# A recurrent attention kernel with a feed-forward part: k and q projected chunk by chunk on one weight load, scores and attends regrouped

## The chip, the cores and the metric

The kernel runs on one core of one Trainium2 chip. The metric is the device time of one execution in microseconds (us).

## The reference

Two parts read the same input `x` (2048 tokens of 1024) and a sigmoid gate mixes them. Part A is recurrent: 64 segments of 32 tokens, each preceded by 8 memory rows that are the first 8 output rows of the segment before.

```python
for s in range(n_seg):                       # 64 segments, one after the other
    h = concat([mem, x[:, 32*s:32*s+32]])    # 8 + 32 rows of 1024
    q, k, v = h @ Wq, h @ Wk, h @ Wv         # 32 heads of 128
    scores = where(mask, q @ k.T * scale, -1e9)
    o = softmax(scores) @ v
    o = o @ Wo
    mem = o[:8]; outs.append(o[8:])
a = concat(outs)
b = (gelu(x @ w_gate) * (x @ w_up)) @ w_down # 1024 -> 3584 -> 1024
out = g * a + (1 - g) * b                    # g = sigmoid(x . gate_w)
```

The comparison with the reference says little about part A. With these inputs `g * a` has a standard deviation of 1.0e-5, the output one of 4.8e-3 (both computed from the reference with and without `Wo`).

## The kernel before

TensorE walks 64 weight chunks of 512 KB in each segment: for each half of the heads eight chunks of k, q, v and o. Most chunks stay in SBUF; twelve places are shared by the two halves ("paired"), so twelve chunks, 6.3 MB, are fetched again in each segment, each as soon as its place has been used. Gaps are filled with projections for later rows ("fills", f1 and f2), which do not hang on the recurrence.

```python
ORDER = (("k", 0), ("q", 0), ("v", 0), ("k", 1), ("q", 1), ("o", 0), ("v", 1), ("o", 1))
walk = [(m, r, i) for m, r in ORDER for i in seq(m, r)]
...
# sharing of bytes that matters below
a_bf = al("a_bf", [128, 256], at=pA.off)      # output rows of a segment; softmax result pA
vA = al("vA", [128, 4, 128], at=oT.off)
tA = al("tA", [128, 8, 32], at=qT.off)        # transposed probabilities
...
def scores(r):                                # TensorE, then the softmax on VectorE
    e.matmul(PB[SS][:, 0:320], lhsT=ident[:, :], rhs=mS..., start=True, stop=False)   # mask
    for lo, hi, c in ((0, 32, 0), (32, 40, 40)):          # 16 main, 16 tail products
        for j in range(4):
            for g in range(4):
                e.matmul(PB[SS][32*g : 32*g+hi-lo, ...], lhsT=qT[:, j, g, :] or qkr[...8 columns],
                         rhs=kT[:, j, g, :], start=False, stop=True)
    ... max, exp, sum, pA = E * 1/sum, tA = transpose(pA), pB, tB = transpose(pB)
...
# projection of a chunk: four 32-column tiles, 512 columns each, a weight load for each
for g in range(4):
    e.matmul(PB[bk][32*g:32*g+32, :], lhsT=h[:, i, :], rhs=w[:, g*512:(g+1)*512], ...)
...
# the second half's place in the segment
on("k", 1, 0, lambda: scores(0))
on("q", 1, 5, lambda: trans(kT))              # after five q chunks
on("o", 0, 0, lambda: evac(bank_of["q", 1], tok))
on("o", 0, 0, some(f1, 2)); on("o", 0, 0, lambda: attend(ua))
on("o", 0, 0, some(f1, 2)); on("o", 0, 0, lambda: attend_tail(ua))
on("o", 0, 0, some(f1, 1)); on("o", 0, 0, lambda: trans(qT))
...
on("o", 1, 3, lambda: fill_store(*k2, G, stage[1]))       # four v_scr stores, if k2 is a v fill
pend.append(store)                            # a_scr <- a_bf, issued early in the next segment
```

Of the kernel before, what the change touches and what calls it, by code (L numbers as in the profile page):

```python
# [195 lines left out]
def bass_gated_mix__memory_aug_recurrent_mem_tr__geglu_ffn__prompt_kernel(  # L196
# [30 lines left out]
    LQ = 40  # L227
    of = out.flatten_outer_dims()
    mem0 = A_mem0.flatten_outer_dims()

    with ExitStack() as es:
# [60 lines left out]
        oT = al("oT", [128, 4, 4, LQ])  # L292
        tok = al("tok", [128, 512])
        stage = [al(f"stg{n}", [128, 512]) for n in range(2)]
# [3 lines left out]
        vA = al("vA", [128, 4, 128], at=oT.off)  # L298
        tA = al("tA", [128, 8, 32], at=qT.off)
# [10 lines left out]
        part = al("part", [128, 256], FP32, at=odd0 + 1024)  # L310
        oR2 = al("oR2", [128, RB, 16], at=odd0 + 1024)
# [5 lines left out]
        def seq(m, r):  # L317
            p = [i for i in range(8) if i in PAIRS[m]]
            f = sorted((i for i in range(8) if i not in p), key=lambda i: (m == "k" and i % 2, i))
            return p + f if r == 0 else f + p  # L320
        ORDER = (("k", 0), ("q", 0), ("v", 0), ("k", 1), ("q", 1), ("o", 0), ("v", 1), ("o", 1))
        walk = [(m, r, i) for m, r in ORDER for i in seq(m, r)]

# [67 lines left out]
        for g in range(4):  # L391
            q = slice(32 * g, 32 * g + 32)


            pw(mS, lambda e, q=q: sel(e, mS[q, 0:NR], ALU.is_ge, NEG, 0, [[-1, NR]], 1))
            pw(mS, lambda e, q=q: sel(e, mS[q, 32:40], ALU.is_ge, NEG, -NR, [[0, NB]], 1))

            pw(mS, lambda e, q=q: sel(e, mS[q, 72:80], ALU.is_ge, NEG, 0, [[-1, NB]], 1))
# [26 lines left out]
        st0 = stage + [al(f"st0{i}", [128, 512], at=odd0 + 1024 * i) for i in range(2)]  # L425
        dl = al("dl", [128, NT], FP32, at=stage[1].off + stage[1].nb - 64)
# [24 lines left out]
        def pre_j(fb, j):  # L451
# [5 lines left out]
            if j == NJP - 1:  # L457
                slow.append(lambda: op("sp", lambda e: e.dma_start(g_scr[fb], g[:, :, :].rearrange("p j c -> p (j c)")), rd=[g.r()],
                                       wr=[("D", "g", fb)], lane=f"gw{fb % 2}"))
# [12 lines left out]
        def load_x(T):  # L472
            if T < NT:
                op("sp", lambda e: e.dma_start(px[T % NPX][:, :], xf[T * 128:(T + 1) * 128, :]), wr=[px[T % NPX].r()], lane=f"px{T % NPX}")
# [52 lines left out]
        load_x(0)  # L527
        op("act", lambda e: e.dma_start(gwb[:, :], gate_w.rearrange("(o d) -> o d", o=1).to_broadcast([128, D])),
           wr=[gwb.r()], lane="gw")
        for T in range(1, NPX):  # L530
            load_x(T)
# [34 lines left out]
        for fb in range(NFB):  # L566
            for j in range(NJP):
                T = TB * (fb + 1) + j
                now, puts[:], slow[:] = list(puts), slow, []
                if T < NT:  # L570
                    do_x(T)
                    load_x(T + NPX)
# [95 lines left out]
        def trans4(e, t=tok):  # L668
            for j in range(4):
                ins = e.transpose(PBV[TT][:, j * 128:(j + 1) * 128], t[:, j * 128:(j + 1) * 128], ident[:, :])  # L670
            return ins

        def trans(to):
            op("pe", trans4, rd=[tok.r(), ident.r()], wr=[BK(TT)])
# [7 lines left out]
        def scores(r, mid=None):  # L682

            def f(e):
                e.matmul(PB[SS][:, 0:320].rearrange("p (a c) -> p a c", a=4), lhsT=ident[:, :],  # L685
                         rhs=mS[:, :].unsqueeze(1).to_broadcast([128, 4, 80]), start=True, stop=False, skip_group_check=True)
                for lo, hi, c in ((0, 32, 0), (32, 40, 40)):
                    for j in range(4):
                        for g in range(4):
                            x = 8 * (4 * j + g)  # L690
                            ins = e.matmul(PB[SS][32 * g:32 * g + hi - lo, j * 80 + c:j * 80 + c + LQ],  # L691
                                           lhsT=qT[:, j, g, :] if lo == 0 else qkr[:, r, 0, x:x + 8], rhs=kT[:, j, g, :], start=False, stop=True, skip_group_check=True)
                return ins
# [24 lines left out]
        def attend(u):  # L718

            def f(e):  # L720
                for j in range(4):
                    for g in range(4):
                        r = slice(32 * g, 32 * g + 32)
                        ins = e.matmul(PB[bo[g]][:, j * LQ:(j + 1) * LQ], lhsT=vA[r, j, :],  # L724
                                       rhs=tA[r, 2 * j:2 * j + 2, :].rearrange("p a c -> p (a c)")[:, 0:LQ],
# [4 lines left out]
        def attend_tail(u):  # L730
            def f(e):
                for g in range(4):
                    r = slice(32 * g, 32 * g + 32)
                    ins = e.matmul(PB[bo[g]][:, 0:4 * LQ].rearrange("p (j c) -> p j c", j=4)[:, :, 24:40], lhsT=vB[r, u, :],  # L734
                                   rhs=tB[r, :, :].rearrange("p (j a) c -> p j (a c)", a=2)[:, :, 24:40],
# [3 lines left out]
            n = 4 * LQ  # L739
            for g in range(4):  # L740
                cp[("act", "dve")[g % 2]](oT[:, g, :, :].rearrange("p j c -> p (j c)"), PB[bo[g]][:, 0:n], [BK(bo[g])],
                                          [oT.r(g * n, (g + 1) * n)])
            op("pool", lambda e: e.tensor_copy(oRc[:, u, :, :].rearrange("p c x -> p x c"),  # L743
                                               oT[:, :, :, 32:40].rearrange("p g j c -> p (g j) c")),
               rd=[oT.r()], wr=[oRc.r(128 * u, 128 * u + 128)])

        bank_of = {("k", 0): B0, ("q", 0): B1, ("v", 0): B2, ("k", 1): B0, ("q", 1): F2, ("v", 1): B0}

        def proj(p, s):
            k = at_step(p, s)  # L750
            w = slots[home[k]]
            i = k[2]
            if k[0] != "o":
                h, bk = hTs[s % 2], bank_of[walk[p][:2]]

                def f(e):
                    for g in range(4):
                        ins = e.matmul(PB[bk][32 * g:32 * g + 32, :], lhsT=h[:, i, :], rhs=w[:, g * 512:(g + 1) * 512],  # L758
                                       start=(p % 8 == 0), stop=(p % 8 == 7))
                    return ins  # L760
                op("pe", f, rd=[h.r(32 * i, 32 * i + 32), w.r()], wr=[BK(bk)])
            else:
# [3 lines left out]
                def f(e):  # L766
                    for hh in range(2):
                        for g in range(4):
                            c = hh * 1024 + g * 256
                            ins = e.matmul(PB[XO][32 * g:32 * g + 32, 0:256], lhsT=oT[:, gp_, 2 * jj + hh, 0:32],  # L770
                                           rhs=w[:, c:c + 256], start=(r == 0 and p % 8 == 0 and hh == 0), stop=(r == 1 and p % 8 == 7 and hh == 1))
                    return ins
                n = 4 * LQ
# [42 lines left out]
        def fill_trans():  # L816
            op("pe", trans4, rd=[tok.r(), ident.r()], wr=[BK(TT)])
# [23 lines left out]
        def tr0(m, u, t, n, G=0):  # L841
            op("pe", lambda e: trans4(e, t), rd=[t.r(), ident.r()], wr=[BK(TT)])
            fill_put(st0[n], "dve")
            if G == 0:
                x = 256 * u + 128 * (m == "k")
                op("pool", lambda e: e.tensor_copy(qkr[:, u, 0 if m == "q" else 1, :], st0[n][:, 0:128]), rd=[st0[n].r(0, 128)],
                   wr=[qkr.r(x, x + 128)])
            fill_store(m, u, G, st0[n])
# [6 lines left out]
        base_of = {mr: 8 * n_ for n_, mr in enumerate(ORDER)}  # L855
# [3 lines left out]
        for s in range(NSEG):  # L859
# [12 lines left out]
            def on(m, r, n, *fs):  # L872
                at.setdefault(base_of[m, r] + n, []).extend(fs)
# [10 lines left out]
            if s == 0:  # L884
                on("k", 0, 0, lambda: mm0("v", 0, F1, st0[3]))
                on("k", 0, 0, lambda: mm0("k", 0, F2, tokB))
                if NG > 1:
                    on("k", 0, 0, lambda: mm0("k", 0, F1, tok, 1, hR1))
                    on("k", 0, 4, lambda: tr0("k", 0, tok, 1, 1))
                on("k", 0, 0, lambda: tr0("k", 0, tokB, 0))  # L890
                on("q", 0, 0, lambda: mm0("q", 0, F1, tokB))
                if NG > 1:
                    def q_next():
                        for f in fill("q", 0, F2, hR1):
                            f()
                        tr0("q", 0, tokB, 2)
                        act_copy(tokB[:, :], PB[F2][:, :], [BK(F2)], [tokB.r()])
                    on("q", 0, 0, q_next)
                    on("q", 0, 3, lambda: tr0("q", 0, tokB, 3, 1))
                else:  # L900
                    on("q", 0, 3, lambda: tr0("q", 0, tokB, 2))
                on("v", 0, 4, lambda: (rest_k(0), load_v(0, slice(0, 1))))

                def fills_1():
# [3 lines left out]
                    tr0("k", 1, tok, 1)  # L908
                    act_copy(tok[:, :], PB[F2][:, :], [BK(F2)], [tok.r()])
                    mm0("v", 1, F1, st0[2])  # L910
                    tr0("q", 1, tok, 3)
# [7 lines left out]
            on("q", 0, 0, lambda: evac(bank_of["k", 0], tok))  # L919
            on("q", 0, 5, lambda: trans(kT))  # L920
            on("v", 0, 0, lambda: evac(bank_of["q", 0], tok))
            on("v", 0, 5, lambda: trans(qT))
            on("k", 1, 0, lambda: evac(bank_of["v", 0], vA))
            on("k", 1, 0, lambda: scores(0))
            on("k", 1, 3, lambda: rest_k(1))
            on("q", 1, 0, lambda: evac(bank_of["k", 1], tok))
            on("q", 1, 5, lambda: trans(kT))

            def add_part():
                op("dve", lambda e: e.tensor_tensor(out=stage[0][:, 0:256], in0=PB[F1][:, 0:256], in1=part[:, :], op=ALU.add),  # L930
                   rd=[BK(F1), part.r()], wr=[stage[0].r(0, 256)])

            on("o", 0, 0, lambda: evac(bank_of["q", 1], tok))
            on("o", 0, 0, some(f1, 2))
            on("o", 0, 0, lambda: attend(ua))
            on("o", 0, 0, some(f1, 2))
            on("o", 0, 0, lambda: attend_tail(ua))
            on("o", 0, 0, some(f1, 1))
            on("o", 0, 0, lambda: trans(qT))
            on("o", 0, 0, some(f1))  # L940
            if k1:
                on("o", 0, 1, lambda: fill_evac(*k1, F1, stage[0]))
# [3 lines left out]
            if k1:  # L946
                on("o", 0, 6, fill_trans)
                on("o", 0, 6, lambda: fill_put(stage[0], "act"))
                on("o", 0, 6, lambda: fill_store(*k1, G, stage[0]))
            if uw == 0:  # L950
                on("o", 0, 6, lambda: store_tail(Q, stage[0]))
            on("o", 1, 0, lambda: evac(bank_of["v", 1], vA))
            on("o", 1, 0, some(f2, 4))
# [190 lines left out]
```

## Time and profile before

| | before |
|---|---|
| median of the first three runs (lowest, highest) | 2238.44 us (2237.15, 2244.4) |
| run with the profile | 2225.83 us, span 2224.0 |
| TensorE busy | 93% of the span |
| first segment ends / recurrence of 62 more / last segment and feed-forward part | 149.8 / 1511.6 / 562.6 us |
| TensorE's waits for instructions ("issue") | 60.0 us |

The recurrence is counted from the closing transposes of the first segment to those of the last; most of the argument is about it. The run with the profile was one of the faster ones, 12 us below the median. Waits: columns are the total in us, the number of waits and the longest.

```profile
DVE pA L704 <- DMA a_scr<-a_bf: 14.4, 16, 1.5
```

The softmax may write `pA` only when the store of `a_bf`, which shares its bytes, has landed. In 16 segments it came too late, and hardly a wait of TensorE follows from it: its waits for kT were 4.5 us in the whole recurrence.

### The profile page before, as it was taken

The numbers are of one execution on the slowest core, as the hardware profiler recorded it, in microseconds if no ns is written. First come the engines' busy times: TensorE is split into PE (matmuls) and PEld (weight loads), VectorE is DVE, ScalarE is ACT, GpSimd is POOL, SyncE is SP. The second block draws the span as 40 slices with busy tenths as digits, with TensorE's granted clock in tenths as the row PEclk, the third lists the DMA queues.
The fourth block names the chain that finished last, engine by engine and source line by source line (L and its number), as shares of the span: only waits on it lengthen the run. The fifth ranks groups of instructions, "written<-read, shape, count | busy, mean of one in ns | idle before, by whom it ended". The sixth has DMA issues, their size and how long they took to land.

```text
span 2224.0 us, 80042 instructions
## 1 busy us (share of the span) xinstructions
PE 2074.7 (93%) x36623; PEld 1096.6 (49%) x36642; DVE 905.1 (41%) x2152; ACT 610.6 (27%) x1296; POOL 617.9 (28%) x1139
## 2 busy tenths in 40 slices
PE   7879999999899999999999999999888999999999
PEld 3334555455555555555555555555444444444444
DVE  5433344334334343443344344334434516354362
ACT  4322322223232232323233232223222303122130
POOL 5123333432333334233333423333321000000000
PEclk9989999999999999999999999999999999999999
DMA  9977888788778888887788788778889410000000
GB/s 321 390 273 278 294 297 290 268 298 305 257 276 299 295 286 280 300 294 279 283 298 297 276 301 302 266 276 323 284 276 366 165 36 29 29 24 34 19 29 19
DMA packets 203440, 529.04 MB, mean 238 GB/s; under 512 B 29592, under 2 KB 46616, under 8 KB 203104
## 3 DMA queue, kind: packets, MB, share of 16 engines
q1 hardware_dynamic: 174064, 471.93, 59.1%
q0 software_dynamic: 28896, 51.75, 7.4%
q8 instruction: 287, 4.70, 0.8%
q10 hardware_dynamic: 144, 0.26, 0.0%
q14 instruction: 49, 0.40, 0.0%
HBM read 490.16 MB, written 33.55 MB: 235 GB/s over the span
## 4 chain that ended last, share of the span: by engine, by line
PE 77%; DMA 10%; POOL 5%; issue 4%; DVE 2%; ACT 1%; SPq 1%; DVEq 0%; POOLq 0%
PE pb L758 25%; PE pb L446 16%; PE pb L770 8%; PE pb L1098 8%; PE pb L785 7%; PE pb L670 4%; PE pb L800 3%; DMA sl<-in_A_Wo_dram 3%; DMA sl<-in_A_Wv_dram 3%; PE pb L691 2%; DMA a_scr<-a_bf 2%; POOL v_scr L826 1%; PE pb L685 1%; PE pb L1080 1%; PE pb L724 1%
## 5 line engine op out<-in xcount | busy, mean ns | idle before, releaser
L758 PE MATMUL pb<-sl,hT 128*32 128x512 bf16 x12288 | 745.9, 381 | 20.9 <-issue 9.7
L758 PEld LDWEIGHTS pb<-sl,hT 128*32 128x32 bf16 x12288 | 330.3, 96 | 285.1 <-issue 17.1
L770 PE MATMUL pb<-sl,oT 128*32 128x256 bf16 x8192 | 282.5, 277 | 44.7 <-issue 38.2
L658 ACT ACTIVATE tok<-pb 128x512 bf16<-128x512 f32 x317 | 189.3, 597 | 398.2 <-PE pb L758 363.1
L743 POOL COPY oRc<-oT 128x128 bf16<-128x128 bf16 x128 | 97.4, 761 | 634.5 <-DVE oT L661 616.1
L770 PEld LDWEIGHTS pb<-sl,oT 128*32 128x32 bf16 x8192 | 209.2, 97 | 95.1 <-issue 50.0
L785 PE MATMUL pb<-sl,hR 128*32 128x512 bf16 x3072 | 226.0, 384 | 6.2 <-DMA sl<-in_A_Wv_dram 4.9
L446 PE MATMUL pb<-xT,wg 128*128 128x512 bf16 x768 | 183.0, 381 | 3.6 <-DMA wg<-in_B_w_gate_dram 3.6
L446 PE MATMUL pb<-xT,wu 128*128 128x512 bf16 x768 | 181.6, 379 | 0.0
L1098 PE MATMUL pb<-wd,GT 128*128 128x512 bf16 x766 | 168.3, 379 | 0.9
L661 DVE CAST oT<-pb 128x160 bf16<-128x160 f32 x256 | 71.2, 320 | 209.4 <-PE pb L734 209.1
L658 ACT ACTIVATE vA<-pb 128x512 bf16<-128x512 f32 x128 | 76.4, 597 | 266.4 <-PE pb L758 266.4
L434 ACT ACTIVATE s<-pb 128x512 f32<-128x512 f32 x112 | 66.9, 597 | 290.4 <-PE pb L446 290.4
L661 DVE COPY kT<-pb 128x512 bf16<-128x512 bf16 x128 | 51.9, 406 | 230.8 <-PE pb L670 88.4
L670 PE MATMUL pb<-ident,tok 128*128 128x128 bf16 x1268 | 126.5, 222 | 8.6 <-DVE kT L661 3.9
L670 PEld LDWEIGHTS pb<-ident,tok 128*128 128x128 bf16 x1268 | 72.3, 98 | 117.2 <-ACT tok L658 88.6
L435 DVE SCALAR_TENSOR_TENSOR tp<-s,pb 128x512 f32<-128x512 f32 x112 | 76.8, 685 | 126.3 <-ACT s L434 125.9
L1098 PEld LDWEIGHTS pb<-wd,GT 128*128 128x128 bf16 x784 | 76.7, 98 | 92.5
L446 PEld LDWEIGHTS pb<-xT,wg 128*128 128x128 bf16 x768 | 75.3, 98 | 95.2 <-issue 5.7
L696 DVE TENSOR_REDUCE st<-pb 128x8 f32<-128x320 f32 x128 | 63.0, 492 | 142.9 <-PE pb L691 142.9
L446 PEld LDWEIGHTS pb<-xT,wu 128*128 128x128 bf16 x768 | 75.3, 98 | 91.0 <-issue 0.8
L1045 POOL DMA_DIRECT2D out_dram<-osb x14 | 7.6, 547 | 372.5 <-PE pb L446 224.6
(96 smaller groups left out, 2146.0 us busy)
## 6 DMA issues: line engine op xcount, KB each, us to landing
sl<-in_A_Wv_dram SPq DMA_DIRECT2D x394, 512.0 KB, 8.8
sl<-in_A_Wo_dram SPq DMA_DIRECT2D x205, 512.0 KB, 6.0
sl<-in_A_Wk_dram SPq DMA_DIRECT2D x142, 512.0 KB, 5.6
sl<-in_A_Wq_dram SPq DMA_DIRECT2D x79, 512.0 KB, 7.1
qkr<-qk_scr POOLq DMA_DIRECT2D x126, 64.0 KB, 2.2
qk_scr<-stg POOLq DMA_DIRECT2D x61, 128.0 KB, 6.0
wd<-in_B_w_down_dram SPq DMA_DIRECT2D x7, 1024.0 KB, 15.7
px<-in_A_x_dram SPq DMA_DIRECT2D x16, 256.0 KB, 6.6
```

What stands on the lines that cost most here:

```text
L434: op("act", lambda e: e.activation(s1[:, :], hg, ACTF.Square, scale=SQ), rd=[BK(bg)], wr=[s1.r()])
L435: op("dve", lambda e: e.scalar_tensor_tensor(out=t[:, :], in0=s1[:, :], scalar=1.0, in1=hg, op0=ALU.add, op1=ALU.mult), rd=[BK(bg), s1.r() ...
L446: ins = e.matmul(PB[bk][:, 0:FB], lhsT=w[:, kc, cc:cc + 128], rhs=x[:, :, :, kc, :].rearrange("p t i c -> p (t i) c"), start=(kc == 0), st ...
L658: op("act", lambda e: e.activation(o, i, ACTF.Copy), rd=rd, wr=wr)
L661: op("dve", lambda e: e.tensor_copy(o, i), rd=rd, wr=wr)
L670: ins = e.transpose(PBV[TT][:, j * 128:(j + 1) * 128], t[:, j * 128:(j + 1) * 128], ident[:, :])
L743: op("pool", lambda e: e.tensor_copy(oRc[:, u, :, :].rearrange("p c x -> p x c"), oT[:, :, :, 32:40].rearrange("p g j c -> p (g j) c")), r ...
L758: ins = e.matmul(PB[bk][32 * g:32 * g + 32, :], lhsT=h[:, i, :], rhs=w[:, g * 512:(g + 1) * 512], start=(p % 8 == 0), stop=(p % 8 == 7))
L770: ins = e.matmul(PB[XO][32 * g:32 * g + 32, 0:256], lhsT=oT[:, gp_, 2 * jj + hh, 0:32], rhs=w[:, c:c + 256], start=(r == 0 and p % 8 == 0 ...
L785: ins = e.matmul(PB[b][32 * g:32 * g + 32, :], lhsT=h[:, k[2], :], rhs=w[:, g * 512:(g + 1) * 512], start=(n == 0), stop=(n == 7))
L800: ins = e.matmul(PB[b][32 * g:32 * g + 32, 0:256], lhsT=t[:, :, 2 * i + hh], rhs=w[:, c:c + 256], start=(ends[0] and i == 0 and hh == 0), ...
L1098: ins = e.matmul(PB[bank[2 * k + hf]][:, :], lhsT=GT[:, j, tb * 128:(tb + 1) * 128], rhs=w[:, jj, hf * 512:(hf + 1) * 512], start=(j == 0) ...
```

## The change

The intent is less TensorE work and fewer instructions. k and q chunks alternate, and q uses the weights that k loaded; the mask product is done in the projections' 32-column tiles; the tail scores are one product for each head group; an attend is one visit instead of two with fills between; one stage buffer remains of two. The prelude's x loads and g stores move to GpSimd's queue, and the feed-forward part's second halves skip their loads too.

```diff
-        ORDER = (("k", 0), ("q", 0), ("v", 0), ("k", 1), ("q", 1), ("o", 0), ("v", 1), ("o", 1))
-        walk = [(m, r, i) for m, r in ORDER for i in seq(m, r)]
+        both = lambda r: [(m, r, i) for i in seq("k", r) for m in "kq"]
+        walk = both(0) + one("v", 0) + both(1) + one("o", 0) + one("v", 1) + one("o", 1)
@@ scores
-                e.matmul(PB[SS][:, 0:320].rearrange("p (a c) -> p a c", a=4), lhsT=ident[:, :],
-                         rhs=mS[:, :].unsqueeze(1).to_broadcast([128, 4, 80]), start=True, stop=False, skip_group_check=True)
+                for g in range(4):
+                    q = slice(32 * g, 32 * g + 32)
+                    e.matmul(PB[SS][q, 0:320].rearrange("p (a c) -> p a c", a=4), lhsT=ident[:, q], ...)
 ... 16 main products as before
+                for g in range(4):
+                    ins = e.matmul(PB[SS][32 * g:32 * g + 32, 0:320]....[:, :, LQ:80],
+                                   lhsT=qkr[:, r, 0, 32 * g:32 * g + 32], rhs=kT[:, :, g, :], ...)
@@ projection
+                        ins = again(e, g, *at, one, end) if k[0] == "q" else e.matmul(*at, start=one, stop=end)
@@ place in the segment
-            on("q", 1, 0, lambda: evac(bank_of["k", 1], tok))
-            on("q", 1, 5, lambda: trans(kT))
-            on("o", 0, 0, lambda: evac(bank_of["q", 1], tok))
-            on("o", 0, 0, some(f1, 2))
+            on("o", 0, 0, lambda: evac(bank_of["k", 1], tok))
+            on("o", 0, 0, lambda: evac(bank_of["q", 1], tok2))
+            on("o", 0, 0, some(f1, 4))
+            on("o", 0, 0, lambda: trans(kT, tok))
+            on("o", 0, 0, some(f1, 2))
+            on("o", 0, 0, lambda: trans_pe(tok2))
             on("o", 0, 0, lambda: attend(ua))
-            on("o", 0, 0, some(f1, 2))
             on("o", 0, 0, lambda: attend_tail(ua))
-            on("o", 0, 0, some(f1, 1))
-            on("o", 0, 0, lambda: trans(qT))
+            on("o", 0, 0, lambda: trans(qT, None))
             on("o", 0, 0, some(f1))
 ... oT 64 columns wide, stage, prelude queues, feed-forward: cut
```

`again` is a matmul without a weight load.

## The prediction

> **What bounds the kernel now.** I read the page first (busy shares, slices, DMA queues), then TensorE's waits, then the timeline of one segment, then the busy shares in 1 us windows. The page says that TensorE is the bound and that, for three quarters of the span, the DMA engines are nearly full too:
>
> ```profile
> PE 2074.7 (93%) x36623; PEld 1096.6 (49%) x36642; DVE 905.1 (41%) x2152; ACT 610.6 (27%) x1296; POOL 617.9 (28%) x1139
> ...
> PE   7879999999899999999999999999888999999999
> ...
> DMA  9977888788778888887788788778889410000000
> ...
> q8 instruction: 287, 4.70, 0.8%
> ```
>
> The span has three stages: a prelude to about 150 us, 63 more recurrent segments to about 1685 us, then the feed-forward part. The transposes of L992 close each segment: first at 149.4 us, last at 1661.2, so a segment takes (1661.2 - 149.4) / 62 = 24.38 us. Nearly all of the change is in the segment. Its parts, from TensorE's timeline (start, length, line):
>
> ```profile
> 1011.66 0.83 PE L758 MATMUL pb<-sl,hT 128*32 128x512 bf16 x12
> 1012.42 0.31 PE L685 MATMUL pb<-mS,ident 128*128 128x320 bf16 x1
> 1012.66 0.28 PE L691 MATMUL pb<-kT,qT 128*32 128x40 bf16 x16
> 1012.77 0.26 PE L691 MATMUL pb<-kT,qkr 128*8 128x40 bf16 x16
> 1012.88 3.00 PE L758 MATMUL pb<-sl,hT 128*32 128x512 bf16 x52
> ...
> 1016.80 0.60 PE L785 MATMUL pb<-sl,hR 128*32 128x512 bf16 x8
> 1017.34 0.27 PE L724 MATMUL pb<-tA,vA 32*128 32x40 bf16 x16
> 1017.54 0.61 PE L785 MATMUL pb<-sl,hR 128*32 128x512 bf16 x8
> 1018.09 0.21 PE L734 MATMUL pb<-tB,vB 32*128 32x64 bf16 x4
> 1018.23 0.40 PE L785 MATMUL pb<-sl,hR 128*32 128x512 bf16 x4
> ```
>
> Lengths overlap, so starts must be read. 52 projection matmuls from 1006.24 lead to a start at 1009.16: 56.2 ns each, 225 ns for the four column tiles of a chunk. TensorE hardly idles here; its waits:
>
> ```profile
> PE pb L770 <- issue: 38.2, 35, 2.5
> PE pb L992 <- ACT a_bf L658: 13.0, 34, 0.4
> PE pb L758 <- issue: 9.7, 13, 1.4
> ...
> PE pb L691 <- issue: 5.0, 5, 1.5
> ```
>
> The rows ending in "issue" add up to 60 us (38.2 + 9.7 + 5.0 + 3.2 + 1.8 + 1.3 + 0.8): waits for no semaphore. Counting TensorE's instructions in the trace in order of time, every such wait over 0.4 us in the recurrence falls at the same place of a run of 256 instructions, 2.2 to 2.6 us after a packet of the instruction queue started. So they are waits for instructions. They come in the output projection and after, where the windows show the DMA share at 0.8 to 1.1 (1011 to 1026 us): the packet then starts 2.5 to 3.7 us after the previous boundary, about 1.1 us early in the segment, and TensorE stands when it has run 256 instructions sooner than that plus 2.4 us.
>
> **What the Trainium skill says.** "TensorEngine Tiling (Array Packing)", section Key Properties: changing the tiling mode drains TensorE. The trace agrees: the mask product, 320 columns on a 128-column tile, between 32-column ones, starts 0.09 us after the projections have streamed and occupies 0.24 us. "TensorE: Matmul & The Clock Gate", section Step-by-step: what each phase is for: a weight load can be pulled ahead of running matmuls. The trace agrees: with a load for each matmul the feed-forward runs 8 matmuls of 512 columns in 1.73 us, 216 ns each. So a removed load is worth little by itself. "Runtime: NRT & Kernel Launch", section Instruction fetch mechanics: blocks of 256 instructions come by the sequencer's own DMA queue, at a cost "mostly hidden". 287 packets of 16 KiB are the 4.70 MB above; that it is hidden does not hold here.
>
> **The change, part by part, per segment.**
> - Scores, twice. Before: 12 matmuls from 1011.66 have streamed at 1011.66 + 12 x 0.0562 = 1012.33 and the next projection starts at 1012.88: 0.55 us. After: the mask product is in the projection's own tile shape, no drain, 320 columns in four tiles at once, some 0.14 us (512 columns take 0.225); the 16 main products 0.11 as now; four tail products of 160 columns for sixteen of 40, about 0.08. Sum 0.33: 0.22 saved, 0.44 for two.
> - Attends, twice. Before: 1017.25 (streamed) to 1017.54 and 1017.99 to 1018.23: 0.53 us with four mode changes. After: one visit, two changes: 0.09 + 0.14 + 0.07 + 0.10 = 0.40. Saves 0.26 for two; the one that follows a transpose directly saves about 0.10 more.
> - q on k's weights: 64 loads go. A chunk costs 225 ns against 216 for one large matmul; if half of this is loads, 16 x 4.5 ns = 0.07 us.
> - The k copy no longer meets a late GpSimd copy (3.9 us over the run): 0.06.
> Saved: 0.93 us.
> - New waits. The q transpose of the second half is now copied by VectorE after the two oT copies, and the second scores follow soon. Before:
>
> ```profile
> 1018.35 0.56 DVE L661 CAST oT<-pb 128x160 bf16<-128x160 f32 x2 [1.11 <-PE pb L734]
> ...
> 1018.99 0.42 DVE L661 COPY qT<-pb 128x512 bf16<-128x512 bf16 x1
> ...
> 1019.87 0.31 PE L685 MATMUL pb<-mS,ident 128*128 128x320 bf16 x1
> ```
>
> There qT is ready 0.46 us early, because 1.8 us of other work lie between attend tail and scores. After, counted from the tail's start: the oT copies start at 0.30 and have 256 columns instead of 160, about 0.34 apart (0.24 now, plus 96 columns at about 1 ns), so qT is copied from 0.98 to 1.40 and seen at 1.46. TensorE has two fill chunks (0.45) and the first output chunk (0.26) to do, and that chunk waits for ScalarE's longer oT copy until about 0.77: it stands before the scores at 1.03. Wait 0.43 us. The longer oT copy costs about 0.12 at each of the two output projections, 0.24. The second transpose waits for the k copy behind softmax in half of the segments: 0.05. Sum 0.72 us lost.
> - Instruction waits, now 60 us / 62 = 0.97 per segment. A segment has 1060 TensorE instructions; 64 + 2 x 18 go (mask 2 to 8, tail 32 to 8), 960 remain, 3.75 blocks instead of 4.14. In the critical stretch (last attend to the next values) 256 instructions take some 0.5 us longer, by 18 fewer instructions and by the new wait itself, so waits of about 1.1 us there become about 0.6, and the later ones (0.6) stay. I put 0.57: 0.40 saved.
> Net 0.93 - 0.72 + 0.40 = 0.61 us, times 63 = 39 us.
> - Prelude: DMA share is over 1.0 from 20 to 110 us, so moving the x loads and g stores to another queue can mostly only fill the weaker 10 to 20 us (0.68): 3 us.
> - Feed-forward: 392 loads go, at most 3.7 ns each (219.7 against 216): 2 us with the small rest.
> Total about 44 us: 2238 - 44 = 2194.
>
> **The rivals.**
> 1. TensorE's saving is real and nothing takes it back: 0.93 x 63 plus 39 us of fewer instruction waits would give about 2140. For it: the waits of before are few. Against: the VectorE order above, which is in the program.
> 2. The weight stream becomes the bound. Twelve fetches of 512 KB a segment land 1.27 us apart in the full stretch, the last values at about 17.4 us of the segment and the last Wo at 21.5; TensorE needs them at about 17.7 and 21.9. Only a few tenths of slack, so a segment 1 us shorter without waits would meet them. Against: the values are now asked for about 0.5 us earlier, since no transpose stands before them, and with the new qT wait TensorE reaches the values no earlier than now. If it binds, 2210.
> 3. The instruction waits do not shrink, as their place is a matter of phase: 2220, with the other terms as above. For: 960 per segment shifts the phase each time. Against: the phase of before covers all places of the segment already, so 0.97 is a fair average.
> 4. No load before a matmul stops the pulling ahead of the next k load: 16 x some 30 ns, 30 us, near 2225. Nothing in the profile before speaks for it.
>
> **Range and chances.** 2193 us. The terms' errors: qT wait +-0.2 us, scores and attends +-0.2, instruction waits +-0.2, each times 63, prelude +-6: together some 25 us. So 2160 to 2225 eight times in ten. The 2% line is 2238.44 x 0.98 = 2193.7, right at the centre: faster 0.50, within 2% 0.47, slower 0.03.
>
> **What would show it.** Segment from 24.4 to about 23.8 us. Scores from 0.55 to about 0.33 us between projections, attend in one block of about 0.40. A wait of about 0.4 us before the second mask product, released by VectorE's qT copy, in nearly every segment, 20 to 30 us in all; and about 0.1 before output chunks, released by oT. "Issue" rows near 35 us. Projection chunks at about 220 ns in pairs. It would be wrong if those qT waits are absent (then faster), if value or Wo waits grow past 10 us, if paired chunks take over 235 ns, or if the prelude changes by more than 10 us.

## The result, and the profile after

| | before | after |
|---|---|---|
| median (lowest, highest) | 2238.01 (2237.15, 2244.4), 4 runs | 2211.91 (2207.04, 2215.16), 4 runs |
| ratio | | 0.9875, 95% interval 0.985 to 0.9901 |
| run with the profile | 2225.83 | 2215.16 |
| first segment ends / recurrence / rest (traces) | 149.8 / 1511.6 / 562.6 | 144.6 / 1503.5 / 565.2 |

A ratio is the mean time of one kernel's runs over that of the other's of the same rounds, so not quite the ratio of the medians. Executions over 1.5% slower than the fastest of the same kernel are left out of the means. The run with the profile was the slowest of the four, and that of before one of the fastest: the two traces are 11 us apart, the medians 26. The change is worth 1.25%, some 26 us: by the 2% line "the same", inside the predicted range, 19 us short of the predicted 2193. Later experiments repeated the changed kernel (2208.07 us, ratio 0.9888).

The busy line, the instruction queue and the chain by engine on the page after:

```profile
PE 2034.4 (92%) x37840; PEld 934.4 (42%) x32178; DVE 931.1 (42%) x2154; ACT 606.9 (27%) x1296; POOL 625.2 (28%) x1155
...
q8 instruction: 274, 4.49, 0.8%
...
PE 60%; DMA 23%; POOL 6%; DVE 6%; issue 3%; ACT 1%; SPq 0%; DVEq 0%; POOLq 0%
```

TensorE lost 40 us of busy time, and the weight loads fell from 36,642 to 32,178, yet the span shrank by 11. The chain that ends last shows where it went: 23% of it are transfers, 10% before. TensorE's waits after, with the same columns as above:

```profile
PE pb L690 <- DVE kT L680: 42.6, 29, 12.2
PE pb L796 <- issue: 22.0, 18, 1.9
PE pb L711 <- DVE qT L680: 17.8, 59, 0.3
PE pb L796 <- DMA sl<-in_A_Wk_dram: 13.7, 18, 1.5
PE pb L1025 <- ACT a_bf L677: 13.0, 34, 0.4
PE pb L807 <- issue: 11.6, 17, 1.5
```

The instruction waits fell from 60.0 to 34.1 us (all "issue" rows), the wait for a_bf is as before, and three are new or have grown: kT (16 us of it in the first segment, 27 in the rest), qT, and the landings of Wk. The parts of a segment, from TensorE's timeline (start, length, instruction, idle time before it with its releaser):

```profile
1006.25 0.40 PE L807 MATMUL pb<-sl,oT 128*32 128x256 bf16 x8
1006.95 0.32 PE L711 MATMUL pb<-mS,ident 128*32 128x320 bf16 x4 [0.30 <-DVE qT L680]
1007.10 0.27 PE L715 MATMUL pb<-kT,qT 128*32 128x40 bf16 x16
1007.20 0.24 PE L718 MATMUL pb<-kT,qkr 128*32 128x160 bf16 x4
1007.27 1.26 PE L807 MATMUL pb<-sl,oT 128*32 128x256 bf16 x40
...
1012.62 0.29 PE L752 MATMUL pb<-tA,vA 32*128 32x64 bf16 x16
1012.75 0.24 PE L762 MATMUL pb<-tB,vB 32*128 32x160 bf16 x4
1012.91 0.61 PE L822 MATMUL pb<-sl,hR 128*32 128x512 bf16 x8
...
1016.94 0.40 PE L796 MATMUL pb<-sl,hT 128*32 128x512 bf16 x4
...
1020.41 1.04 PE L796 MATMUL pb<-sl,hT 128*32 128x512 bf16 x16
```

The scores take 1007.27 - 1006.95 = 0.32 us, as predicted (0.33); the attend and its tail 1012.91 - 1012.62 = 0.29 plus the change of mode before them. Sixteen k and q chunks lie between 1016.94 and 1020.41: 217 ns each. The prediction read 225 before, from 52 products up to the start of the transposes, and so counted a change of tile mode in: the thirteenth of those chunks starts at 1008.84, 12 x 216.7 ns after the first, so the distance of chunks did not change. The qT wait is there, in 59 segments, 0.30 instead of 0.43 us.

Where does the kT wait of a segment come from? The chain through one of them, in order of time (start, us, what):

```profile
1044.77 8.04 DMA a_scr<-a_bf
...
1052.90 0.44 DVE pA L732
...
1053.36 0.45 DVE tA L734
...
1054.32 0.40 DVE kT L680
1054.71 0.04 issue
1054.76 0.56 PE pb L690 x4
1055.32 0.33 PE pb L752 x16
```

The store of the last segment's rows lands after 8.04 us; only then may the softmax write pA; the kT copy stands behind the softmax in VectorE's order; the second transposes need the bank that it empties. VectorE's row for this grew:

```profile
DVE pA L732 <- DMA a_scr<-a_bf: 34.0, 27, 3.1
```

To have one sum for all traces I took TensorE's waits of more than 0.06 us out of the recurrence (62 segments between the first and last closing transposes). What is left is TensorE's own work:

| us in the recurrence | before | after | after, second trace |
|---|---|---|---|
| own work | 1411.5 | 1374.4 | 1371.7 |
| instruction waits | 60.6 | 34.0 | 31.6 |
| kT | 4.5 | 26.7 | 23.5 |
| qT | 0.7 | 17.6 | 18.0 |
| Wk | 0 | 13.7 | 13.3 |
| oT | 3.1 | 3.9 | 3.9 |
| all waits | 100.2 | 129.1 | 122.7 |

Own work fell by 37 to 40 us, instruction waits by 27 to 29, and 52 to 56 us of other waits came.

Own work has to be read with the clock that was granted in the recurrence: 0.997 before, 0.991 and 0.994 in the two traces after. Own work times this clock is 1405 to 1407 us in the two traces of the old order (before and, below, e11_before_store). In the ten traces of the changed program, e7_mask and e8_nov left out, it is 1362 to 1367, though own work itself goes from 1369.6 to 1390.3. So differences of a few us in own work below, and most of the 12 us of e5_qload_shift and e6_copies, go with the clock.

### The profile page after: what moved, and what is told of

Same layout as the page of the kernel before. It is cut to its first block, busy times and chain, and to the rows that moved or that the text cites. A ratio compares the mean times of both kernels' runs of the same rounds, so it can differ in the third digit from the quotient of the medians.

```text
span 2213.4 us, 76738 instructions
## 1 busy us (share of the span) xinstructions
PE 2034.4 (92%) x37840; PEld 934.4 (42%) x32178; DVE 931.1 (42%) x2154; ACT 606.9 (27%) x1296; POOL 625.2 (28%) x1155
## 4 chain that ended last, share of the span: by engine, by line
PE 60%; DMA 23%; POOL 6%; DVE 6%; issue 3%; ACT 1%; SPq 0%; DVEq 0%; POOLq 0%
PE pb L462 16%; PE pb L796 11%; PE pb L779 8%; PE pb L807 7%; DMA a_scr<-a_bf 7%; DMA sl<-in_A_Wk_dram 6%; PE pb L822 5%; DMA sl<-in_A_Wv_dram 4%; PE pb L1135 4%; PE pb L690 3%; DMA sl<-in_A_Wo_dram 3%; POOL v_scr L863 2%; DVE oT L680 2%; DMA xr_scr<-xr 2%; PE pb L837 1%
## 5 line engine op out<-in xcount | busy, mean ns | idle before, releaser
L796 PE MATMUL pb<-sl,hT 128*32 128x512 bf16 x8192 | 665.0, 381 | 48.6 <-issue 22.0
L779 PE MATMUL pb<-sl,hT 128*32 128x512 bf16 x4096 | 398.0, 379 | 0.0
L796 PEld LDWEIGHTS pb<-sl,hT 128*32 128x32 bf16 x8192 | 210.5, 96 | 429.7 <-issue 274.5
L677 ACT ACTIVATE tok<-pb 128x512 bf16<-128x512 f32 x318 | 176.3, 596 | 346.1 <-PE pb L796 320.6
L822 PE MATMUL pb<-sl,hR 128*32 128x512 bf16 x3072 | 209.9, 384 | 0.0
L680 DVE CAST oT<-pb 128x256 bf16<-128x256 f32 x256 | 96.7, 419 | 182.9 <-PE pb L762 182.9
L1135 PE MATMUL pb<-wd,GT 128*32 128x512 bf16 x1568 | 152.2, 379 | 0.0
L779 PE MATMUL pb<-wd,GT 128*32 128x512 bf16 x1568 | 152.2, 379 | 0.0
L677 ACT ACTIVATE oT<-pb 128x256 bf16<-128x256 f32 x256 | 84.3, 381 | 189.9 <-PE pb L762 189.9
L726 ACT ACTIVATE E<-pb 128x320 bf16<-128x320 f32 x128 | 56.0, 438 | 220.5 <-DVE pb L725 220.5
```

Source lines behind the costliest of these rows:

```text
L677: op("act", lambda e: e.activation(o, i, ACTF.Copy), rd=rd, wr=wr)
L680: op("dve", lambda e: e.tensor_copy(o, i), rd=rd, wr=wr)
L779: return e.add_instruction(mybir.InstMatmult(name=nc.get_next_instruction_name(), start_tensor_calc=start, stop_tensor_calc=stop, tile_siz ...
L796: ins = again(e, g, *at, one, end) if k[0] == "q" else e.matmul(*at, start=one, stop=end)
L822: ins = e.matmul(PB[b][32 * g:32 * g + 32, :], lhsT=h[:, k[2], :], rhs=w[:, g * 512:(g + 1) * 512], start=(n == 0), stop=(n == 7))
L1135: ins = again(e, q, *a, j == 0, j == NJ - 1) if hf else e.matmul(*a, start=(j == 0), stop=(j == NJ - 1))
```

## The experiments

Theory at the start: the changed kernel's gain is eaten by three waits (the late a_bf store, VectorE's order ahead of qT, the place of the instruction blocks), and each can be taken away alone. Rival: TensorE's time is no longer what sets the segment, so a wait removed in one place comes back in another. The first four, the next four, then three, then the last were each made together on one chip, beside runs of the kernel before; where the changed kernel was not among them, the ratios to the kernel before are compared.

**The changed kernel again.**

> The changed kernel again, unaltered, as the measure for the three runs beside it. Expected 2212 us, 0.9875 of the kernel before within 0.003; segment mean 24.2 to 24.3 us; instruction waits 30 to 38 us in all; wait of the second mask product for qT near 18 us, of the second transposes for kT near 27 us in the recurrence (42.6 with the prelude), for Wk near 14 us.

Measured: 2208.07 us, 0.9888 (0.9866 to 0.9909); issue rows 31.5, kT 37.8 in all, qT 18.1, Wk 12.8. This is the measure for the next three.

**The early store (e1_store).** The a_bf store is issued before the four v_scr stores.

```diff
-                if k2[0] == "v":
-                    on("o", 1, 3, lambda: fill_store(*k2, G, stage))
@@ store, run early in the next segment
                 op("pool", ... a_scr[s] <- a_bf ...)
-                if k2 and k2[0] == "q":
+                if k2:
                     fill_store(*k2, G, stage)
```

> The a_bf store goes out ahead of the four v_scr stores on GpSimd's queue, in the segments that have them. Theory (the second transposes wait for kT because VectorE's softmax may not write pA, which shares its bytes with a_bf, until that store has landed, 10.4 to 11.8 us into the segment): the store is issued at about 1.7 instead of 3.9 us and lands before 9.9 us, so the pA waits (34 us) and the kT waits inside the recurrence (27 us) nearly vanish; since some of it then meets the DMA-bound Wv and Wo landings, the time falls by 10 to 25 us against the changed kernel run beside it. Rival (the kT copy is late only because VectorE is busy with the rest of the softmax, store or not): kT waits stay above 20 us and the time within 4 us.

Measured: 2193.06 us, 0.9815 (0.9796 to 0.9834), so 0.9815 / 0.9888 = 0.9926 of the changed kernel, 16 us. VectorE's waits have no row for the store any more. TensorE's:

```profile
PE pb L796 <- issue: 21.9, 18, 1.7
PE pb L711 <- DVE qT L680: 19.4, 64, 0.3
PE pb L796 <- DMA sl<-in_A_Wv_dram: 18.1, 27, 1.2
PE pb L690 <- DVE kT L680: 17.2, 7, 11.0
```

The theory holds: kT fell by 20 us (3.1 are left in the recurrence; the rest is the first segment). 13 us came back as waits for Wv (5.4 in the changed kernel). All waits of the recurrence together fell from 122.7 to 111.2 us.

**The qT copy between the oT copies (e2_qt).**

```diff
             for g in range(4):
+                if mid and g == 3:
+                    mid()                      # VectorE's qT copy
                 cp[("act", "dve")[g % 2]](oT[:, g, ...], PB[bo[g]]...)
```

> VectorE copies qT between its two oT copies instead of after both. Theory (the 0.30 us wait ahead of the second scores is only the order on VectorE): the qT copy ends about 0.37 us sooner, the wait of 17.8 us goes to about 0, the last oT copy is 0.42 us later and is needed only three output chunks on, so at most 3 us come back there; the time falls by 12 to 18 us against the changed kernel. Rival (the time saved is waited out again at the Wv and Wo landings or for instructions): the qT wait goes, the value, Wo and issue waits grow by as much, and the time falls by less than 5 us.

Measured: 2207.24 us, 0.9878 (0.9857 to 0.99): no gain. The wait did not move, only its name:

```profile
PE pb L711 <- DVE oT L680: 17.8, 59, 0.3
```

Neither theory nor rival. The fourth attend bank is the scores bank (`bo = (B0, B1, B2, SS)`), so the mask product must wait for its oT copy too. Whichever of VectorE's three copies is last ends the wait.

**The q loads restored (e3_qload).**

```diff
-                        ins = again(e, g, *at, one, end) if k[0] == "q" else e.matmul(*at, start=one, stop=end)
+                        ins = e.matmul(*at, start=one, stop=end)
```

> The q projections load their weights again, as before the change; the order k, q, k, q stays. Reading of the trace (without the load both chunks of a pair take 216 ns, with it both take 225): 32 chunks of 9 ns or 0.29 us a segment, 18 us in the run, and 64 more instructions a segment add 5 to 10 us of instruction waits: 20 to 28 us slower than the changed kernel. The prediction (half of the 9 ns, on the q chunks alone: 0.07 us a segment): 4 us plus the instruction waits, some 10 us. Its rival 4 (an unloaded matmul hinders the next load): faster with the loads back.

Measured: 2203.18 us (2183.91 to 2213.11), 0.9845 (0.9806 to 0.9884): not slower, perhaps a little faster, with a wide spread. The first two expectations missed; the third has the sign, but not the reason. Own work rose by 6.1 us (1377.8 against 1371.7), but the clock granted in the recurrence was 0.991 instead of 0.994, and own work times the clock rose by 1 us. The first 12 chunks of a segment are 216.8 ns apart in both traces. So no cost of the loads shows, and neither my reading of the trace (0.29) nor the prediction's 0.07 holds. What did change are the instruction waits, which fell, though each segment has 64 instructions more:

```profile
PE pb L807 <- issue: 18.8, 15, 2.9
...
PE pb L752 <- issue: 1.7, 4, 0.6
...
PE pb L762 <- issue: 0.7, 1, 0.7
```

With two smaller rows they add up to 21.9 us, against 31.5. Rival 4 of the prediction (an unloaded matmul hinders the next load) would also make it faster with loads, but the equal 216.8 ns speak against it. The count gives another reason. TensorE's instructions in four segments, semaphore instructions included: 4242 before, 3838 after, 4094 here. In blocks of 256 that is 16.57, 14.99 and 15.99: before the change the block boundaries pass through all places of the segment, and in the two others they stay where they are. In the traces of the changed kernel each of the 14 segments with s mod 4 = 1 that has all its fills waits for instructions, at the same place (693 to 719 instructions into the segment, 2 later each time), 0.7 to 1.9 us.

The next four runs, on another chip, tried this and the qT wait.

**The place of the blocks, changed kernel (e4_phase).** 44 idle transposes at the start of TensorE's program.

```diff
+        def shift(e):
+            for _ in range(44):
+                ins = e.transpose(PBV[TT][:, 0:128], ident[:, :], ident[:, :])
+            return ins
+        op("pe", shift, rd=[ident.r()], wr=[BK(TT)])
         op("pe", tr_mem, ...)
```

> The changed kernel with 44 idle transposes (88 TensorE instructions, loads included) at the very start of TensorE's program, where it waits for data anyway; nothing else. Theory (the instruction waits depend on where the 256-instruction boundaries fall in the segment; the changed kernel has 3838 TensorE instructions in four segments, 2 short of 15 blocks, so its boundaries stay at one place, and that is a bad one: every segment with s mod 4 = 1 waits 1.0 to 1.9 us): 88 more move each boundary 88 instructions earlier. Replaying the trace's instruction times with each block arriving 3.5 us after the boundary before it (5.3 to 5.7 us between 12 and 23 us of the segment) gives 4 to 16 us of waits at the new place against 27 to 48 at the present one; so the issue rows fall from 32 to 5 to 15 us, the time by 10 to 25 us against the changed kernel. Rival (the waits depend on the number of instructions and the DMA load only): issue rows stay at 28 to 38 us, the time within 4 us.

Measured: 2223.58 us (2220.7 to 2226.66), 0.9937 (0.9922 to 0.9953): about 0.55% slower than the changed kernel's 0.9875 and 0.9888 elsewhere. Issue rows 38.1. The waits moved by the 88 instructions, as the theory says (607 to 633 instead of 693 to 719), so the place matters, but my replay of it failed: one wait of about 1.4 us became one or two of 0.5 to 1.2 us, and the segments with s mod 4 = 2 now wait too. The blocks of this stretch are all near their limit, and a shift trades one against the next.

**The place of the blocks, with q loads (e5_qload_shift).** As e3_qload with 64 idle transposes.

> The kernel with the q loads restored (e3_qload) and 64 idle transposes (128 instructions) at the very start. e3_qload has 4094 instructions in four segments, 2 short of 16 blocks, so its boundaries are locked too, and by the same replay they lie at nearly the best place (6 to 21 us of waits; its trace has 22) while 128 instructions earlier is the worst (52 to 88 us). Theory of the place: issue rows of 45 to 80 us and the time 25 to 50 us above that of e3_qload, which is the same program but for the idle transposes. Rival (number and load only): issue rows at 18 to 28 us, time as e3_qload within 5 us.

Measured: 2239.21 us (2228.96 to 2249.95), 1.001 (0.9981 to 1.0039), against 0.9845 without the idle transposes: 1.7%, some 37 us, for instructions that do nothing in a place where TensorE idles.

```profile
PE pb L801 <- issue: 27.7, 30, 1.9
...
PE pb L812 <- issue: 16.0, 20, 1.5
```

Issue rows 44.9 us against 21.9 (just under the range), and kT in the recurrence 42.9 against 12.1. The time is in the expected range; only 23 of the 37 us are instruction waits by name. The recurrences of the two traces are 46 us apart: issue adds 23, kT 31 and own work 12.5, while the landings of Wk, Wv and Wo take off 19. Own work times the clock is the same to 2 us (1367 and 1365): the granted clock was lower, 0.978 to 0.985 in all six runs, 0.987 to 0.991 in those of e3_qload. So the place of the blocks is shown to double the instruction waits, but not to be the whole of the 37 us; why the clock was lower and why the kT waits follow was not tested.

**ScalarE takes three of the oT copies (e6_copies).**

```diff
-            for g in range(4):
-                cp[("act", "dve")[g % 2]](oT...)
+            for g in first:                    # (0, 3, 1, 2) in the first attend
+                cp[on[g]](oT...)               # ("dve", "act", "act", "act")
```

> After the first attend, VectorE makes the oT copy of bank 0 and then the qT copy; ScalarE makes the other three, that of the scores bank first. e2_qt showed that the second mask product waits for whichever of VectorE's three copies is last, since one of them reads the scores bank. Theory (the wait is VectorE's three copies in a row): with two in a row qT is ready about 0.37 us sooner, the wait ahead of the mask product (18 us) falls to 0 to 4 us, and the output chunks after the scores wait for ScalarE's last copies at most 0.1 us (6 us in all); the time falls by 5 to 15 us against the changed kernel. Rival (the end of the segment is set by the Wv and Wo landings and the instruction blocks, which the saved 0.3 us does not move): the mask wait goes, other waits grow as much, and the time falls by less than 5 us.

Measured: 2228.69 us (2215.89 to 2236.99), 0.9956 (0.9931 to 0.9981): 0.7 to 0.8% slower than the changed kernel, some 16 us. The wait ahead of the scores is gone (qT has no row), so the theory of its cause is right, and the rival of its worth is right and more:

```profile
PE pb L690 <- DVE kT L680: 43.9, 29, 11.1
PE pb L807 <- issue: 39.0, 33, 2.8
PE pb L796 <- issue: 19.9, 17, 2.3
```

Instruction waits 59.8 instead of 31.5 us. In segments with s mod 4 = 1 TensorE reaches the same boundary sooner and waits 2.1 us instead of 1.4. The edit also adds one semaphore instruction a segment, so the boundaries drift the other way; the two effects are not separated. Own work is 12 us longer as well, 9 of them by a lower clock (0.988 against 0.994 in the recurrence), whose cause is open.

**The mask product whole again (e7_mask).**

```diff
-                for g in range(4):
-                    q = slice(32 * g, 32 * g + 32)
-                    e.matmul(PB[SS][q, 0:320]..., lhsT=ident[:, q], ...)
+                e.matmul(PB[SS][:, 0:320]..., lhsT=ident[:, :], ...)
```

> The mask product as one matmul of 128 columns again, as before the change; the rest as changed. The prediction's term (no drain of the tile mode: 0.33 us to 0.14 us for the mask part): the visit of the scores takes 0.19 us longer, twice a segment, 24 us in the run. Since 12 instructions a segment fewer make the block boundaries rotate (3790 in four segments), the instruction waits should be 25 to 35 us spread over all segments instead of fixed to those with s mod 4 = 0 and 1. Rival (the drain is small, the gain of the scores is in the tail products): the visit grows by less than 0.08 us, the time by less than 10 us.

Measured: 2206.1 us (2203.4 to 2208.56), 0.9863 (0.9845 to 0.9882): not slower at all. Yet the scores did get longer:

```profile
1005.50 0.31 PE L709 MATMUL pb<-mS,ident 128*128 128x320 bf16 x1 [0.31 <-DVE qT L680]
1005.74 0.28 PE L713 MATMUL pb<-kT,qT 128*32 128x40 bf16 x16
```

0.24 us from the mask to the main products instead of 0.15, and own work of the recurrence is 1389.6, 18 us more than the changed kernel, 0.29 us a segment (0.38 expected). The waits took it back: issue 24.4, kT 14.9 and Wk 6.8 us in the recurrence, 22 less together. So here 18 us more of TensorE's work cost no time. But the edit also sets the boundaries moving (3790 instructions in four segments, 14.80 blocks), and how much of the 22 us comes from that and how much from the longer visits was not separated.

**Half of the weight stream (e8_nov).** If neither work nor single waits set the time, the DMA engines remain. This kernel does not fetch the paired v chunks again; its TensorE program is the same, its result wrong.

```diff
-            if done[n] < len(uses[n]) and uses[n][done[n]] != k:
+            if done[n] < len(uses[n]) and uses[n][done[n]] != k and k[0] != "v":
                 fetch(n)
```

> The changed kernel without the re-fetches of the six paired Wv chunks (the result is wrong on purpose; TensorE's program, the waits in it and the instruction count stay). Theory (instruction blocks, the a_bf store and the Wk and Wo landings are all late because 6.3 MB of weights a segment fill the DMA engines; TensorE's own work does not set the time of the recurrence): with half of that stream gone the issue rows fall from 32 to below 8 us, the kT waits inside the recurrence from 24 to below 5, Wk, Wv and Wo waits from 22 to below 3; the qT wait (18) and the a_bf wait (13) stay; the time falls by 60 to 80 us, to 2130 to 2150. Rival (an instruction block takes its 3.5 to 5.7 us whatever the DMA engines carry; the kT wait is VectorE's): issue rows stay above 20 us and kT above 15, the time falls by 20 to 35 us.

Measured: 2142.55 us (2138.2 to 2145.72), 0.959 (0.9568 to 0.9613). It was called correct, which shows only how little the comparison sees of part A; 10 Wv fetches are in the trace instead of 394. The DMA line, 40 slices of the span in tenths, and TensorE's waits:

```profile
DMA  9945545545555555555555554555569100000000
```

```profile
PE pb L711 <- DVE qT L680: 18.8, 62, 0.3
PE pb L690 <- DVE kT L680: 17.4, 9, 10.7
PE pb L1025 <- ACT a_bf L677: 13.0, 34, 0.4
PE pb L807 <- DMA sl<-in_A_Wo_dram: 12.1, 19, 1.8
PE pb L796 <- DMA sl<-in_A_Wk_dram: 10.7, 21, 1.2
```

With the DMA share at a half instead of eight tenths, the instruction waits are 1.3 us in all, kT 3.0 in the recurrence, and own work is 14 us less, some 12 of it at equal clock. So it is the full DMA engines that make the instruction blocks late, not their own length. For the store this is not shown: its median from issue to landing is 6.9 us here, 7.0 and 7.3 in the traces of the changed kernel, and between 2 and 7 us of a segment, most of its way, the DMA engines are as full here (0.93 to 1.01) as there. The stores issued after 3 us land 0.5 us sooner (6.4 against 6.9 and 7.0), and VectorE's wait for them is 5.4 instead of 34 us. The theory's size held (65 us), but Wk and Wo did not vanish: TensorE now comes earlier to them.

**The memory keys' copy in the first segment (e9_store_rest).** As e1_store, and:

```diff
                     tr0("k", 0, tokB, st0[0])
+                    rest_k(0)                  # ahead of the chain of qk_scr stores
@@
-                on("v", 0, 4, lambda: rest_k(0))
```

> The early a_bf store (as e1_store) and, in the first segment only, GpSimd's copy of the memory keys into kT ahead of the chain of qk_scr stores, each of which waits for the one before (5 to 6 us each). Theory: the 11 to 12 us wait of the second transposes at 115 us of the span goes, but the Wv loads of the start, which the kernel before waited for 5 us there, come out from behind it; the first segment ends 4 to 9 us sooner, time 2184 to 2190 us. Rival (the first segment is set by the Wv and vB landings): it ends within 2 us of where it did, time as e1_store, 2193.

Measured: 2198.19 us, 0.984 (0.9819 to 0.986). The first segment ends at 143.8 instead of 145.4 us; kT fell to 8.6 us, and the waits for Wv rose to 21.6. The rival holds: nothing gained, the ratio is no better than that of e1_store.

**Early store and q loads (e10_store_rest_q).** e9_store_rest with the edit of e3_qload.

> As e9_store_rest, with the q loads restored as in e3_qload (4094 instructions in four segments, boundaries at the place with the fewer waits). If place of the boundaries and store add up: issue rows 18 to 28 us instead of 31, kT in the recurrence below 4, and 2 to 12 us under e9_store_rest, though TensorE has some 6 us more work. Rival (sooner arrival at the block boundaries or at the Wk and Wv landings takes the gain): issue and Wk rows grow above those of e3_qload (22 and 23 us), time equal to or above e9_store_rest.

Measured: 2185.51 us (2177.09 to 2211.41), 0.9794 (0.9753 to 0.9835): the lowest median of all correct versions, but one of its six runs was at 2208 and one, at 2211, was listed as slow (the median of the five others is 2182.67), and its interval overlaps that of e1_store. Issue 20.9 and kT 3.1 in the recurrence are as if the two edits added up, Wk stays at 24.9. Both e1_store and this one beat the kernel before and the changed one.

**The early store in the kernel before (e11_before_store).** The last question was whether the store is a fault of the change or was there all along.

> The kernel before, with the a_bf store ahead of the four v_scr stores and nothing of the change. Theory (the store was as late in the kernel before, but its wait of 14 us on VectorE lay under TensorE's q projections, which came between the k transposes and the attend; the change took that cover away): the time stays within 4 us of the kernel before, VectorE's wait for the store falls from 14 us to below 4, TensorE's waits for kT, 4.5 us in the recurrence, stay below 5, and its instruction waits stay at 50 to 70 us, since 4242 instructions in four segments let the boundaries pass through all places. Rival (an early store is worth 15 us in any kernel, by taking a transfer out of the full stretch): 10 to 18 us faster than the kernel before.

Measured: 2230.2 us, 0.9985 (0.9959 to 1.0011): nothing to tell apart from the kernel before.

```profile
DVE pA L704 <- DMA a_scr<-a_bf: 0.4, 1, 0.4
```

VectorE's wait went from 14.4 to 0.4 us and the time stayed. The late store was in the kernel before, under cover; the change uncovered it. It also made it somewhat later: from issue to landing the store takes 6.1 us in the median before (6.2 here) and 7.0 and 7.3 after. This trace is also a second one of the old order: own work 1411.9, instruction waits 57.1 us in the recurrence, within 4 us of the first.

## Why the prediction was right in its range and high in its size

It gave "faster" and "the same" nearly even chances; the range held, the centre was 19 us too low. Its terms per segment, beside what the runs showed:

| term | predicted | measured | from |
|---|---|---|---|
| own work saved (scores, attends, q loads) | 0.87 | 0.60 to 0.64; at equal clock 0.63 to 0.72 | own work, 37 to 40 us (39 to 45) / 62 |
| of it q loads | 0.07 | none seen | 216.7 ns a chunk before, 216.8 after and in e3_qload |
| of it mask product | 0.38 | 0.29 | e7_mask |
| of it tails and attends | 0.42 | 0.3 to 0.4 | what is left |
| qT wait | +0.43 | +0.28 | 17.6 us / 62 |
| longer oT copies | +0.24 | +0.01 | oT row |
| kT (saved 0.06, lost 0.05) | -0.01 | +0.36 | kT row, 4.5 to 26.7 us |
| Wk landings | not in the sum | +0.22 | Wk row |
| instruction waits | -0.40 | -0.43 | issue rows |

1. *The step that failed* is "The second transpose waits for the k copy behind softmax in half of the segments: 0.05." The mechanism was named, its size was not worked out from what holds the softmax up: the a_bf store, which VectorE's row of before already showed with 14 us. e1_store gives back 16 us by moving that store alone, and e11_before_store shows that the same move was worth nothing before.
2. The saving in own work had the right mechanism and nearly the right size. In the timelines of all segments (medians, the last chunk's 0.217 taken off) an attend with its tail takes 0.39 us instead of 0.53 (0.40 predicted), and the first scores 0.30 instead of 0.55 (0.33 predicted). Only the q loads are worth nothing; their 0.07 came from the 225 ns, a misreading. The two waits that were not foreseen in size (kT, Wk) cost 0.59 us more than predicted, and two foreseen ones (qT, oT copies) 0.38 less; that the total came as near as it did is partly luck.
3. The Wk landings are in no term; rival 2 looked at values and Wo only. The third chunk fetched in a segment was a q chunk before, wanted 10.5 us into the segment; now it is a k chunk, wanted at 9.5 us. It lands at about the same time, at 9.2 us in the median before and 9.3 after, so in 18 segments it is late.
4. The instruction waits fell by the predicted amount, but the reason given (fewer instructions, all places equally likely) is not what the runs show. More instructions had fewer waits (e3_qload), and idle ones in the prelude brought 23 us more of them (e5_qload_shift). Rival 3 of the prediction was right that the place is what counts, and wrong that it covers all places: after the change it is locked.
5. Rival 2 was right in a wider sense than it was written. The weight stream does bind, and not through the values alone: without half of it the instruction waits are gone (e8_nov).
6. Prelude: 5.2 us sooner (3 predicted). Feed-forward: 2.6 us later in the traces instead of 2 sooner. The prediction's "392 loads go" is wrong: since all blocks came out in 32-column tiles, the down products have 1568 loads instead of 784. It made little difference: a down visit of the first blocks takes 48.5 us, 48.3 before. Most of the rest is the first up projection, which starts 1.6 us later, after a longer wait for w_gate (5.0 against 3.6 us).

Still open: why kT waits follow the place of the blocks in e5_qload_shift, how much of e6_copies' loss is drift of the boundaries, why these two were granted a lower clock, and what in e7_mask took the added work back.

## What to carry to other kernels

When TensorE is at 93% and the DMA engines at 80% at the same time, a saving on TensorE is only an upper bound: e7_mask added 18 us of work and lost no time, e6_copies removed 18 us of wait and lost 16 (both also moved the boundaries of the instruction blocks). Before a stretch of work is moved or shortened, list what it covers, from the waits of the engines that are not the bound; a row of 14 us on VectorE that cost nothing became 22 us on TensorE. And where "issue" waits are large, count the instructions between their places: a difference between two versions may be the place of a block boundary, which idle instructions in the prelude can test. Compare the granted clock of the two versions as well before a difference in TensorE's work is called a result.

## What the Trainium skill lacked or had wrong

- "Runtime: NRT & Kernel Launch", section Instruction fetch mechanics, calls the cost of a block "mostly hidden". Here TensorE waited 60.0 us for instructions before and 34.1 after, up to 2.8 us at a time (e6_copies); with the weight stream halved it was 1.3 us (e8_nov). The page has nothing on the place of the boundaries: 128 idle instructions in the prelude doubled these waits, from 21.9 to 44.9 us (e3_qload, e5_qload_shift).
- "TensorEngine Tiling (Array Packing)", section Key Properties, says that a change of the tiling mode drains TensorE, without a size. Two mask products a segment in 128-column instead of 32-column tiles cost 0.29 us of TensorE's work (e7_mask), about 0.15 us each, the difference in streaming included.
- "TensorE: Matmul & The Clock Gate", section Step-by-step: what each phase is for, tells that loads can be pulled ahead, not what leaving one out is worth. Here nothing shows: chunks of four products of 512 columns are 216.8 ns apart with a load for each product (e3_qload) and without loads for every second chunk (after).
- No page was found with a figure for the delay of a small store among large loads: the a_bf store took 7.0 us from issue to landing in the median after, 9.1 at most, with the DMA engines' share at 0.9 or above from 2 us of a segment on.
